# Later weight loads, and queries of the second batch loaded by token, in a one-core attention and MLP kernel

## The chip, the cores and the metric

The kernel runs on one core of one Trainium2 chip. The metric is the device time of one execution in microseconds (us). The core has five engines that run side by side, each in the order of its own program: TensorE (PE in the profile, its weight loads PEld), VectorE (DVE), ScalarE (ACT), GpSimd (POOL) and SyncE (SP). DMA transfers are issued from SyncE's and GpSimd's queues, and all of them run on the same 16 DMA engines.

## The reference

There are 4 batches of 8 heads, 768 tokens and 64 dimensions. The tokens are cut into 8 blocks of 96. A small matrix per head, made doubly stochastic by five Sinkhorn rounds, mixes the key and value blocks; each query block then attends to its mixed key block alone. The result, as 768 tokens of 512 channels, goes through a residual MLP: one matrix over tokens, one pair of matrices over channels.

```python
P = sort_net
for _ in range(5):
    P = P - np.max(P, axis=-1, keepdims=True)
    P = np.exp(P)
    P = P / (np.sum(P, axis=-1, keepdims=True) + 1e-09)
    P = P / (np.sum(P, axis=-2, keepdims=True) + 1e-09)
k_sorted = np.einsum('bhij,bhjcd->bhicd', P, k_b)      # v_sorted in the same way
scores = scale * np.matmul(q_b, k_sb.transpose(0, 1, 2, 4, 3))
attn = softmax(scores)                                 # per row, written out in the reference
x = np.matmul(attn, v_sb)                              # then heads side by side: (4, 768, 512)
a1 = alpha1 * x + beta1
u = x + lam * np.einsum('ts,bsd->btd', w_tok, a1)
a2 = alpha2 * u + beta2
out = u + lam * (np.maximum(a2 @ w_ch1, 0.0) @ w_ch2)
```

## The kernel before

**Order.** Every engine's instructions keep the order in which the program emits them (lines 55 to 77). Dependencies between engines, and the reuse of buffers, are guarded by semaphores that the framework sets. A tile is taken from a pool under a tag with a fixed number of copies; a new tile of a tag waits until the last reader of the tile whose place it takes is done, also when that reader stands later in the program than the new tile.

**Start-up (lines 96 to 319 and 900 to 989).** GpSimd issues the loads of batch 0: q in slabs (`load_slabs`, line 117: a partition holds 12 tokens of one head in one piece), v in halves of 64 partitions (`load_halves`, line 122), k in slabs, then the four loads of `w_tok` (lines 156 to 170). Meanwhile VectorE and ScalarE make the Sinkhorn matrix (lines 302 to 319); the table `beside` (line 293) lists what is emitted after each of the five rounds: `heads` (two small constant tables on ScalarE), the turning of q by TensorE (`q_first`), its copies out (`q_out`), and `slow`, a matmul on zeros that only keeps TensorE running. From line 900 the sorted v is laid out by copies (`v_sort`) on GpSimd and ScalarE and mixed, then k, then scores (`score`), weighted sums (`pv_first`), the permutation and transposition of `w_tok` (`permute`, `prep_wtok`), and the token matrix of batch 0 (`first_mm`, `first_turn`). `first_turn` needs `brow`, the product of beta and lam in one row (line 944), copied to three further partitions by SyncE.

**Batches.** A batch's MLP runs in two halves (`hf` 0 and 1) of 384 tokens. A half has 16 hidden units (`h_unit`, kind "h") and then product steps (`ch_unit` or `ch_pair`, kind "c"). The work of the next batch's attention is hung between them: `put(b, hf, kind, n, f)` emits `f` after hidden unit or product step `n` of half `hf` of batch `b`. The attention of batch 1 lies in batch 0: the mixing of v and k (`mix_v`, `mix_k`) at the end of the first half, scores and weighted sums (`pv`) between the hidden units of the second half, from (0, 1, "h", 0) on. The mixing of batch 2 lies in the product steps (0, 1, "c", 0) to (0, 1, "c", 7).

**Loads of the later batches.** `load_kv` (line 195) loads v, then k, in halves, into the tag `raw`, which has two copies. `load_q` (line 185) loads q into the tag `qn`, which has one: batch 1 in slabs (two DMAs), batches 2 and 3 by tokens (six DMAs; a partition is a token, in 64-element pieces per head). q of batch 1 is turned by TensorE in `q_turn_late` (line 538), 24 matmuls of 64 by 64 and two copies by VectorE for each of four groups of two heads, at product steps 4, 5, 7 and 8 of batch 0's first half; q of batches 2 and 3 is turned by transposing DMAs on SyncE (`q_cross`). `loads(2)` stands at (0, 0, "c", 11). It begins with a one-element copy on GpSimd from Vs (`gate`), which waits until the mixed v of batch 1 is back from its way through DRAM (`bounce_v` out, `back_v` in).

## Time and profile before

| | us |
|---|---|
| runs | 256.35, 256.37, 257.83 (median 256.37) |
| profiled execution | 256.33 |
| its span | 254.6 |
| DVE busy | 174.1 |
| ACT busy | 155.7 |
| POOL busy | 46.1 |
| q of batch 1, turned by TensorE: first to last group | 58.2 to 64.5 |
| `gate` of batch 2's loads | 69.2 |
| first mix of batch 2's v | 84.8 |

All the engine times are from one profiled execution and count from the start of its span. In the profile's lines, `out<-in` are the program's tile names without numbers, and all work has line 65, the helper that records every instruction, so lines are told apart by tile names: `raw` is a tile of v or k, `qn` and `q8b` of q, `wt` and `wp` of w_tok, `sc_ps` of scores, `x_ps` of weighted sums, `mix_ps` and `kmix_ps` of the mixing, `h_ps` of hidden units, `ch_ps` of products. A line of the timeline gives start, duration, engine, operation, tiles and shapes, the count, and in brackets the idle time before it with what ended it. A line of windows gives the stretch, its length, busy time and instructions of PE, PEld, DVE, ACT and POOL, the granted clock of TensorE, the DMA share and GB/s.

### The profile page before, as it was taken

To read this page: it belongs to the slowest core of one execution; us is meant where nothing else is said; L and a number is where in the kernel's file an instruction comes from. 1 tells how busy PE (TensorE), PEld (TensorE's weight loads), DVE (VectorE), ACT (ScalarE), POOL (GpSimd) and SP (SyncE) were. 2 spreads that over 40 slices of the span, in tenths; PEclk is the share of its full clock that TensorE was granted. 3 is DMA by queue.
4 is the path that set the end of the run, shared out by engine and by line. 5 is a ranking of instruction groups with operands and counts; after the bars stand their busy time and mean duration, and the time that the engine had idled before them with its cause. 6 is when DMAs were issued, how large, how long until landed. Compare 5 with 4: busy or idle time off the path is not lost.

```text
span 254.6 us, 6059 instructions
## 1 busy us (share of the span) xinstructions
PE 244.0 (96%) x2416; PEld 159.7 (63%) x2416; DVE 174.1 (68%) x461; ACT 155.7 (61%) x285; POOL 46.1 (18%) x70
## 2 busy tenths in 40 slices
PE   7897999999999999999999999999999999999994
PEld 2475765555465545556765797558756875686783
DVE  5884588667379868279896685398978862462773
ACT  4796675567788679786564696878364005837400
POOL 8699604000082010191000010000000000000000
PEclk9997999999999999999999999999999999999999
DMA  5999999998999997999961179710203132111023
GB/s 98 202 210 192 207 205 210 216 179 197 165 179 180 131 209 124 178 159 164 136 161 39 31 189 127 141 23 0 85 0 66 50 115 45 21 41 44 0 85 82
DMA packets 61936, 31.09 MB, mean 122 GB/s; under 512 B 50562, under 2 KB 57618, under 8 KB 61908
## 3 DMA queue, kind: packets, MB, share of 16 engines
q0 software_dynamic: 20976, 16.91, 45.7%
q1 hardware_dynamic: 40836, 13.76, 32.0%
q8 instruction: 19, 0.31, 0.5%
q14 instruction: 9, 0.07, 0.1%
q10 hardware_dynamic: 96, 0.03, 0.1%
HBM read 32.79 MB, written 8.65 MB: 163 GB/s over the span
## 4 chain that ended last, share of the span: by engine, by line
PE 77%; DVE 9%; ACT 6%; DMA 3%; issue 2%; POOL 1%; DVEq 0%; ACTq 0%; POOLq 0%
PE h_ps L65 28%; PE tok_ps L65 12%; PE px L65 8%; PE ch_ps L65 8%; PE pz L65 6%; PE py L65 5%; DMA v<-in_v_dram 3%; PE x_ps L65 3%; DVE x L65 3%; PE sc_ps L65 2%; DVE sums L65 2%; PE kmix_ps L65 2%; PE mix_ps L65 2%; ACT kT L65 1%; ACT vd L65 1%
## 5 line engine op out<-in xcount | busy, mean ns | idle before, releaser
L65 PE MATMUL h_ps<-a2T,W1p 128*128 128x384 bf16 x512 | 93.4, 326 | 0.3 <-DVE a2T L65 0.3
L65 PEld LDWEIGHTS <-W1p 128*128 128x128 bf16 x512 | 47.8, 98 | 30.7
L65 ACT ACTIVATE hTa<-h_ps 128x384 f16<-128x384 f32 x64 | 31.2, 490 | 30.6 <-PE h_ps L65 29.5
L65 ACT ACTIVATE hTb<-h_ps 128x384 f16<-128x384 f32 x64 | 31.3, 489 | 8.7 <-PE h_ps L65 8.7
L65 DVE SCALAR_TENSOR_TENSOR u<-tok_ps,x 128x512 f32<-128x512 f32 x21 | 14.5, 692 | 27.0 <-PE tok_ps L65 27.0
L65 PE MATMUL tok_ps<-a,w_tokT 128*128 128x512 f16 x126 | 30.3, 379 | 0.0
L65 ACT CAST kT<-kmix_ps 64x512 f16<-64x512 f32 x36 | 25.7, 713 | 7.0 <-PE kmix_ps L65 6.5
L65 ACT ACTIVATE et<-sc_ps 96x768 f16<-96x768 f32 (+2 forms) x36 | 24.6, 736 | 2.4 <-PE sc_ps L65 2.4
L65 ACT CAST u<-u 128x512 f16<-128x512 f32 x21 | 13.0, 618 | 20.4 <-DVE u L65 20.4
L65 PEld LDWEIGHTS <-sums 128*128 128x128 f16 x216 | 21.1, 98 | 3.8 <-issue 0.7
L65 PEld LDWEIGHTS <-hTa 128*128 128x128 f16 x192 | 18.2, 98 | 6.6
L65 PEld LDWEIGHTS <-hTb 128*128 128x128 f16 x200 | 18.5, 98 | 6.1
L65 PEld LDWEIGHTS <-w_tokT 128*128 128x128 f16 x126 | 12.3, 98 | 13.1 <-DVE a L65 0.3
L65 DVE TENSOR_TENSOR x<-x_ps,rcb 96x512 f16<-96x512 f32 x24 | 16.5, 687 | 0.8
L65 DVE TENSOR_TENSOR sums<-hTa,hTb 128x512 f16<-128x512 f16 (+2 forms) x27 | 8.9, 330 | 10.3 <-ACT hTb L65 10.0
L65 PEld LDWEIGHTS <-et 96*128 96x128 f16 (+4 forms) x288 | 12.6, 103 | 2.7
L65 DVE SCALAR_TENSOR_TENSOR ost<-px,u 128x256 f32<-128x256 f32 x27 | 11.3, 419 | 3.4 <-PE px L65 3.4
L65 PE MATMUL x_ps<-Vs,et 96*128 96x65 f16 (+4 forms) x288 | 13.5, 199 | 0.0
L65 PE MATMUL ch_ps<-W2p,hTa 128*128 128x512 f16 x48 | 11.9, 380 | 0.0
L65 PE MATMUL ch_ps<-W2p,hTb 128*128 128x512 f16 x48 | 11.7, 379 | 0.0
L65 POOL DMA_DIRECT2D qn<-in_q_dram x12 | 10.7, 915 | 5.2 <-DMA raw<-in_v_dram 4.8
L65 PE MATMUL sc_ps<-qT,kT 64*128 64x96 f16 (+1 forms) x256 | 10.0, 210 | 1.5 <-DVE x L65 0.7
(140 smaller groups left out, 351.2 us busy)
## 6 DMA issues: line engine op xcount, KB each, us to landing
out_dram<-ost SPq DMA_DIRECT2D x23, 192.0 KB, 2.4
raw<-in_v_dram POOLq DMA_DIRECT2D x6, 384.0 KB, 8.4
raw<-in_k_dram POOLq DMA_DIRECT2D x6, 384.0 KB, 10.8
Vs<-vscr SPq DMA_DIRECT2D x3, 768.0 KB, 7.9
W1p<-in_moe_w_ch_dram POOLq DMA_DIRECT2D x4, 512.0 KB, 11.6
W2p<-in_moe_w_ch_dram POOLq DMA_DIRECT2D x4, 512.0 KB, 15.6
qn<-in_q_dram POOLq DMA_DIRECT2D x12, 128.0 KB, 11.1
vscr<-mixed POOLq DMA_DIRECT2D x4, 384.0 KB, 5.0
```

Of the source, the lines that this page charges most:

```text
L65: ins = getattr(self.eng, name)(*args, **kwargs)
```

## The change

It has five parts. The loads of `w_tok` become a function that is called after GpSimd's value sorts. The table `beside` is reordered: `heads` one round later, one `slow` moved behind the mixing of keys. The product for `brow` and its copies move behind the loads of alpha, beta and lam, two W1 loads and the first permutation; `pv_first(1)` moves ahead of group 2's scores. v of batch 1 is loaded ahead of the last part of W2, and the scaling of that part moves from hidden unit 12 to 15. And q: batch 1's is loaded by tokens, as batches 2 and 3 are, and turned by six 128-column transposes and one copy per group, the first at product step 10, the others after hidden units 1, 3 and 5 of the second half; for batch 2, q is issued ahead of v and k.

```diff
--- before.py
+++ after.py
@@ -154,19 +154,19 @@
     load_halves(v8, v[0])
     load_slabs(k8, k[0])
     wt16 = []
-    for half in range(2):
-        t_ = att.tile([128, 3, S], F16, name="wt16", tag=("sums", "qn")[half], bufs=(2, 1)[half])
-        for lo, n in ((0, 96), (TAIL, 32)):
-            pool.dma_start(
-                t_[lo // 6:lo // 6 + n],
-                moe_w_tok[lo + 3 * half * n:lo + 3 * (half + 1) * n, :].rearrange("(tt p) s -> p tt s", p=n),
-            )
-        wt16.append(t_)
-        if half == 0:
-            pool.memset(VD[:, :, HB:64], 0.0)
-            pool.memset(
-                KT0[:].rearrange("p g i (th t) -> p (g i th) t", th=2)[:, :, HB:64].bitcast(FT), 0.0
-            )
+
+    def load_wt():
+        for half in range(2):
+            t_ = att.tile([128, 3, S], F16, name="wt16", tag=("sums", "qn")[half], bufs=(2, 1)[half])
+            for lo, n in ((0, 96), (TAIL, 32)):
+                pool.dma_start(
+                    t_[lo // 6:lo // 6 + n],
+                    moe_w_tok[lo + 3 * half * n:lo + 3 * (half + 1) * n, :].rearrange("(tt p) s -> p tt s", p=n),
+                )
+            wt16.append(t_)
+
+    pool.memset(VD[:, :, HB:64], 0.0)
+    pool.memset(KT0[:].rearrange("p g i (th t) -> p (g i th) t", th=2)[:, :, HB:64].bitcast(FT), 0.0)
 
     def v_sort(lo, hi, eng):
         eng(VD[:, lo:hi, 0:HB], v8[:, :, lo:hi].rearrange("p t d -> p d t"))
@@ -183,17 +183,15 @@
     qn_of = {}
 
     def load_q(b):
-        if b == 1:
-            qn_of[b] = att.tile([128, H4, 12 * D], F16, name="q8b", tag="qn", bufs=1)
-            return load_slabs(qn_of[b], q[b])
         qn_of[b] = att.tile([128, NT, H, D], F16, name="qn", tag="qn", bufs=1)
         for kt in range(NT):
             pool.dma_start(
                 qn_of[b][:, kt, :, :], q[b, :, kt * 128:(kt + 1) * 128, :].rearrange("h p d -> p h d"),
             )
 
-    def load_kv(b):
-        for kv, src in ((1, v), (0, k)):
+    def load_kv(b, *kvs):
+        for kv in kvs or (1, 0):
+            src = (k, v)[kv]
             raw = att.tile([128, HB, D], F16, name="raw", tag="raw", bufs=2)
             load_halves(raw, src[b])
             raw_of[(b, kv)] = raw
@@ -254,7 +252,7 @@
     def q_turn(b, g, ps):
         if g == 0:
             qT_of[b] = att.tile([128, H4, S], F16, name="qT", tag="qT", bufs=1)
-        return turn_slab(qn_of[1] if b else q8, lambda r, g: ident16[r, r], g, "q_ps", ps)
+        return turn_slab(q8, lambda r, g: ident16[r, r], g, "q_ps", ps)
 
     def q_copy(b, g, ps, half, eng):
         eng(
@@ -291,11 +289,11 @@
             q_copy(0, g, qps[g], half, act.copy)
 
     beside = {
-        0: [heads, lambda: q_first(0), lambda: q_first(1)],
-        1: [lambda: slow(1), lambda: q_first(2)],
-        2: [lambda: q_out(0), lambda: slow(1)],
-        3: [lambda: q_out(1), lambda: q_out(2, 0), lambda: q_first(3), lambda: slow(1)],
-        4: [lambda: q_out(2, 1), lambda: q_out(3), lambda: prep_ab2(psb), lambda: gaps()],
+        0: [lambda: q_first(0), lambda: q_first(1)],
+        1: [heads, lambda: slow(1), lambda: q_first(2)],
+        2: [lambda: q_out(0), lambda: q_first(3)],
+        3: [lambda: q_out(1), lambda: slow(1)],
+        4: [lambda: q_out(2), lambda: q_out(3), lambda: prep_ab2(psb), lambda: gaps()],
     }
     slow(2)
     warm(1)
@@ -536,16 +534,25 @@
         )
 
     def q_turn_late(g):
-        ps = q_turn(1, g, psb)
-        q_copy(1, g, ps, 0, dve.tensor_copy)
-        q_copy(1, g, ps, 1, dve.tensor_copy)
+        if g == 0:
+            qT_of[1] = att.tile([128, H4, S], F16, name="qT", tag="qT", bufs=1)
+        ps = psb([128, S], F16, "qt_ps")
+        for kt in range(NT):
+            pe.transpose(
+                ps[:, kt * 128:(kt + 1) * 128],
+                qn_of[1][:, kt, 2 * g:2 * g + 2, :].rearrange("p a d -> p (a d)"), ident16[:],
+            )
+        dve.tensor_copy(qT_of[1][:, g, :], ps[:])
 
     gate = const([1, 1], F16, "gate")
 
     def loads(b):
         pool.tensor_copy(gate[:], Vs[0:1, 0, 0:1])
+        if b == 2:
+            load_q(b)
         load_kv(b)
-        load_q(b)
+        if b > 2:
+            load_q(b)
 
     mixed = {}
 
@@ -900,9 +907,11 @@
     mix_values(0, psb)
     warm(1)
     mix_keys(0, psb)
+    slow(1)
     v_sort(48, 64, pool.tensor_copy)
     v_sort(40, 48, pool.tensor_copy)
     v_sort(32, 40, pool.tensor_copy)
+    load_wt()
     for n in range(4):
         v_sort(8 * n, 8 * n + 8, act.copy)
 
@@ -941,19 +950,21 @@
     score(0, 1, 0, psb, 1)
     score(0, 1, 1, psb)
     prep_scales()
-    pool.tensor_tensor(brow[0:1, :], bet1[:], lam1[:], ALU.mult)
-    for j in range(1, 4):
-        sp.dma_start(brow[32 * j:32 * j + 1, :], brow[0:1, :])
     pool.dma_start(alphaB[:], moe_alpha1.partition_broadcast(128))
     pool.dma_start(betaB[:], moe_beta1.partition_broadcast(128))
     pool.dma_start(lamB[:], moe_lam.partition_broadcast(128))
     for g in range(2):
         pool.dma_start(W1p[:, :, g * 512:(g + 1) * 512], w1v[:, :, g * 512:(g + 1) * 512])
     permute(0, pool.tensor_copy, 0, 6)
+    pool.tensor_tensor(brow[0:1, :], bet1[:], lam1[:], ALU.mult)
+    for j in range(1, 4):
+        sp.dma_start(brow[32 * j:32 * j + 1, :], brow[0:1, :])
     for g in range(2, 4):
         pool.dma_start(W1p[:, :, g * 512:(g + 1) * 512], w1v[:, :, g * 512:(g + 1) * 512])
     permute(1, pool.tensor_copy, 0, 6)
     for g in range(4):
+        if g == 3:
+            load_kv(1, 1)
         pool.dma_start(W2p[:, g * 4:(g + 1) * 4, :], w2v[:, g * 4:(g + 1) * 4, :])
     moe_start(0)
     a1_of[0] = moep.tile([128, 8, C], F16, name="a1", tag="a1", bufs=1)
@@ -963,9 +974,9 @@
     for g, kp in ((2, kp2), (3, kp3)):
         k_copy(0, g, kp, 0, copy)
         k_copy(0, g, kp, 1, act.copy)
+    pv_first(1)
     score(0, 2, 0, psa)
     score(0, 2, 1, psb)
-    pv_first(1)
     score(0, 3, 0, psb)
     score(0, 3, 1, psa)
     for ks in range(4):
@@ -984,7 +995,7 @@
     first_turn(2, psa)
     scale_affine(betaB)
 
-    load_kv(1)
+    load_kv(1, 0)
     load_q(1)
     pool.memset(Vs[0:BLK, :, D:GRP], 1.0)
 
@@ -1020,7 +1031,7 @@
             put(0, 0, "h", 15, lambda: bounce_v(1))
             put(0, 0, "c", 2, lambda: back_v(1))
             for g in range(H4):
-                put(0, 0, "c", (4, 5, 7, 8)[g], lambda g=g: q_turn_late(g))
+                put(0, min(g, 1), *(("c", 10), ("h", 1), ("h", 3), ("h", 5))[g], lambda g=g: q_turn_late(g))
             put(0, 0, "c", 11, lambda: loads(2))
             seq = [("s", 0), ("s", 1), ("s", 2), ("p", 0), ("s", 3), ("p", 1), ("p", 2), ("s", 4), ("p", 3), ("s", 5),
                    ("p", 4), ("s", 6), ("p", 5), ("s", 7), ("p", 6), ("p", 7)]
@@ -1058,7 +1069,7 @@
         put(b, 0, "h", 4, lambda b=b: moe_cross(b, 1))
         put(b, 0, "c", 2, lambda b=b: moe_affine(b, 1))
 
-    for g, m in enumerate((10, 11, 12, 12)):
+    for g, m in enumerate((10, 11, 12, 15)):
         put(0, 0, "h", m, lambda g=g: scale_weights(g))
     for n, at_ in enumerate(((0, 1, "c", 4),) * 3 + ((0, 1, "c", 5),) * 3 + ((0, 1, "c", 6),) * 2):
         put(*at_, lambda n=n: block_weights(n))
```

## The prediction

> **What bounds the kernel now.** I read the page first, then windows over the stages the change touches, then the timelines of GpSimd, SyncE and TensorE there. Two lines of the page, busy time and granted clock:
>
> ```profile
> PE 244.0 (96%) x2416; PEld 159.7 (63%) x2416; DVE 174.1 (68%) x461; ACT 155.7 (61%) x285; POOL 46.1 (18%) x70
> ...
> PEclk9997999999999999999999999999999999999999
> ```
>
> TensorE is busy for 244.0 of 254.6 us and works in program order. From about 22 us on, whatever it waits for lengthens the run, and what other engines save does not shorten it. The one dent is in the first 27 us; the windows there (engine busy time, then granted clock, DMA share, GB/s):
>
> ```profile
> 19.80:21.20 1.40, 0.00 (x0) 0.00 (x0) 1.02 (x2) 0.50 (x2) 1.40 (x2) 1.00 1.21 200
> ...
> 23.00:26.30 3.30, 3.30 (x55) 2.89 (x51) 1.50 (x4) 2.60 (x6) 3.30 (x4) 0.51 1.18 223
> ```
>
> TensorE stood still for 1.4 us, and soon afterwards ran 3.3 us at a granted clock of 0.51. In the stretch 19.3 to 22.6, one such length before, it was busy 0.44 + 0 + 0.94 + 0.07 = 1.45 of 3.3 us (44%). In 9 to 13 us it was busy about 80% and stayed at 1.00.
>
> The batch-2 loads, on GpSimd's queue:
>
> ```profile
> 69.19 0.18 POOL L65 COPY gate<-Vs 1x1 f16<-1x1 f16 x1 [25.74 <-DMA Vs<-vscr]
> ...
> 69.80 1.08 POOL L65 DMA_DIRECT2D raw<-in_v_dram  x2 [0.43 <-issue]
> 70.86 1.06 POOL L65 DMA_DIRECT2D raw<-in_k_dram  x2
> 71.87 3.61 POOL L65 DMA_DIRECT2D qn<-in_q_dram  x4
> 76.48 0.88 POOL L65 DMA_DIRECT2D qn<-in_q_dram  x1 [0.99 <-DMA raw<-in_v_dram]
> 78.85 0.87 POOL L65 DMA_DIRECT2D qn<-in_q_dram  x1 [1.49 <-DMA raw<-in_v_dram]
> ```
>
> The gate opens when batch 1's values are back in Vs; then v, k and q go out in that order. Their users on TensorE, from its timeline:
>
> ```profile
> 73.42 0.82 PE L65 MATMUL h_ps<-a2T,W1p 128*128 128x384 bf16 x4
> ...
> 84.78 0.59 PE L65 MATMUL mix_ps<-raw,bigM 128*128 128x512 f16 x2
> ...
> 87.80 0.61 PE L65 MATMUL kmix_ps<-bigP,raw 128*128 128x128 f16 x8
> ```
>
> The mix of v at 84.78 comes 14.4 us after the second v load was issued (70.34), the mix of k at 87.80. This cover is what the change spends. The last view is the stage before it, where q of batch 1 is turned today:
>
> ```profile
> 58.23 0.57 PE L65 MATMUL q_ps<-ident,q8b 64*64 64x64 f16 x24
> ...
> 68.88 0.34 PE L65 MATMUL sc_ps<-qT,kT 64*128 64x96 f16 x7 [0.43 <-ACT kT L65]
> ```
>
> **Start-up.** The four w_tok loads (0.56 to 0.69 us of issue each, 2.5 in sum) move behind GpSimd's three value sorts, which end at 15.1. GpSimd idled 2.2 us before those sorts, so the issue was free and now is not: the alpha, beta and lam rows and W1 go out about 2.5 us later. The transfers themselves are in one line: q landed at 6.0 and 8.0, v at 10.0 and 11.9, k at 14.8 and 16.6, w_tok at 19 to 22. So v, which starts the critical sorts at 12.0, was not held by w_tok behind it: 0 gained (bounds 0 and the 2.2 us that GpSimd waited for v; I take 0, as v's landing follows q's at q's pace). A load issued at 15.1 moves its first bytes about 2 us later (q: issued 1.27, traffic from 3), so the DMA engines stay idle for about 0.5 us after k and every later load shifts by that. First w_tok lands near 20; the permutation starts at 20.9 instead of 19.9 and ends at 23.1, while its transposes run at 25.4: hidden by 2.3 us. If that cover went, each us late would cost a us. The brow product (1.26 us) moves behind that permutation, to 24.4; its three copies need 1.9 us to issue and 4.9 to land, so the last lands near 30.5, against its first use at 30.24: +0.3, bounds 0 and 1.5 (copies each a full 4.9 after a late product).
>
> The heads leave the Sinkhorn chain (its Exp waited for them from 4.12 to 4.69), but v at 11.9 still ends last: 0. One 1.1-us filler matmul is moved behind the mixing of keys, where TensorE waits for sorted v until 12.98: 0 (bounds 0 and 0.6). The weighted sum of group 1 goes ahead of group 2's scores and fills the 0.4-us wait before 22.54: -0.4. Start-up: **-0.1**.
>
> **Loads of batch 1.** v goes ahead of the last W2 part, which lands some 4 us later, near 50.5; its scaling starts at 53.8 today and its first matmul at about 56: hidden. q by tokens moves in 64-element pieces. The q loads of batch 2 show their pace: 155 GB/s in 80 to 86 us, against 207 around 35 us. For 0.79 MB this is 5.1 instead of 3.8 us, so q lands near 59 instead of 57.3. Its first transpose comes at about 64: hidden by 5 us. GpSimd issues six loads of 0.91 instead of two of 0.74 us, with nothing urgent behind them. The bounce of batch 1's v (SyncE, 55.05) and its way back (61.22, 7.9 us to landing) share the engines with q and may land 0 to 2 us after 69.1; the weighted sum that needs it comes at about 70.9: 0, bounds 0 and 1.
>
> **Turning q.** A group's 24 matmuls pushed the next product from 58.14 to 58.73, 0.59 us. Six transposes: three of w_tok's push the next matmul by 0.16 us (36.80 to 36.96), so 0.33 for six; with weight loads of 0.098 us fully exposed, 0.59. I take 0.4. Four groups leave the first product stage before its last mix of k: 4 x 0.59 = 2.36. ScalarE's key copies are freed as early (third set at 63.6, second set done at 63.4), so kT is complete at 66.5 instead of 68.8 and scores start 2.36 earlier. Three groups return in the next stage: 3 x 0.4 = 1.2. VectorE trades eight copies of 0.548 us, idle time there, for four of about 0.55 (w_tok's 384 columns took 0.29 to 0.36); three fall into 70 to 80 us, where it is busy 8.39 of 10 us, and 1.65 us of work fits 1.61 of room: +0.2, bounds 0 and 1. Sum: -2.36 + 1.2 + 0.2 = **-1.0**. TensorE would reach the mix of v at 83.8.
>
> **q ahead of v and k in batch 2.** This adds a wait. The buffer of q has one copy, and its last reader is now batch 1's fourth turn, after the sixth hidden unit: 73.42 + 0.65 - 2.36 + 0.8 + 0.4 + 0.2 = 73.1 us. GpSimd stands at the first q load until then, and queued behind it are five q loads, then v, then k. Six issues take 5.4 us; the second v load goes out 6.0 us after 73.1 instead of at 70.34: 8.8 us later. TensorE has 83.8 - 73.1 = 10.7 us. Landing of v from issue: 5.1 us (shortest raw load) to 8.4 (median), so 11.1 to 14.4 us after 73.1: a stall of 0.4 to 3.7. By the whole transfer: v, k and q took from 69.8 until the traffic fell at 86,
>
> ```profile
> 85.00:86.00 1.00, 1.00 (x6) 0.49 (x5) 0.97 (x3) 0.59 (x1) 0.00 (x0) 1.00 3.39 144
> 86.00:87.00 1.00, 1.00 (x7) 0.45 (x5) 0.95 (x3) 0.72 (x2) 0.00 (x0) 1.00 0.36 23
> ```
>
> 16.2 us. Begun at 73.1 it ends at 89.3, now with k, needed at 86.8: a stall of 2.5. The two ways give 2.5 to 3.7; I take **3.0**, bounds 0.4 and 5 (a gate 1 us later as well). SyncE's transposes of q no longer wait for q, but batch 2's scores only begin at 102.8, so that gains nothing.
>
> **Sum.** -0.1 - 1.0 + 3.0 = +1.9 us on the profiled run's 256.33 (span 254.6 and 1.7 around it; the median shown is 256.37): **258.2 us**, if the stall leaves the clock alone.
>
> **Rivals.**
> B, half clock after the stall: a 3.0-us standstill in a 3.3-us stretch leaves TensorE busy for as little as 10%, or some 55% in each of two stretches if it straddles them; 44% was followed by 3.3 us at 0.51 above, 80% was not. TensorE is fully loaded in 87 to 91 us, so such a stretch costs 3.3 x 0.49 = 1.6 us: 259.8, slower. It decides once the stall takes over half of a stretch. [...]
>
> C, the early half-clock stretch vanishes: with the filled gap TensorE is busy about 1.9 of 3.3 us (57%) before 22.6, between the 44% and the 80%. Gain 1.6: 256.6.
>
> D, v and k land in time (5.1 us from issue, k close behind): 255.2. For it: loads of one queue landed strictly in turn at start-up. Against: the second v load took 8.4 us even when nothing of its queue but v was ahead.
>
> E, the later w_tok does not clear the way but starves the start: if the DMA engines idle until 18 to 19 us and brow lands late, start-up costs 2 to 2.5 us more: 260.5.
>
> **Chances.** A (forecast) 0.38, B 0.22, C 0.14, D 0.13, E 0.08, C and D together (253.6) 0.05. A's own range, from its bounds, is 256 to 260. The range reaches from the lower part of D to the upper part of E; C with D, the ends of D and E, and B with a longer stall are left out, about 2 in 10: **254.5 to 260.8**. About 1% (2.6 us) is what a measurement of this kernel can tell from no change. Faster by more, below 253.8: C with D and the low edge of D, 0.07. Slower, above 258.9: B, E and the upper quarter of A, 0.39. Within: 0.54.
>
> **What would show it.** In the changed profile: GpSimd's gate near 69 and its first batch-2 q load not before 73; second v load near 79; TensorE idle 2 to 4 us at the first mix of v or k of batch 2, released by a load; a slice below 9 in the clock row near 88 us for B, none near 24 us for C; scores of batch 1 near 66.5; brow's copies near 24.5 and the first turn within 0.5 us of 30.2. I am wrong if that idle time is under 1 us, or if the first hidden unit, at 33.0 today, moves by over 1 us.

## The result, and the profile after

The changed kernel takes **264.98 us** (median of 6 runs, 263.59 to 265.82) against 256.48 us (median of 6 runs, 256.28 to 257.83) for the kernel before: a ratio of 1.031, 95% interval 1.028 to 1.034. That is 8.5 us slower. The prediction was 258.2 us, with 260.8 as its upper end: too fast by 6.8 us, and outside the range. The profiled execution took 264.54 us, with a span of 262.8 us.

On the page, the busy times and the clock row answer to the two lines shown of before:

```profile
PE 245.6 (93%) x2344; PEld 160.0 (61%) x2344; DVE 173.2 (66%) x457; ACT 155.9 (59%) x285; POOL 50.2 (19%) x74
...
PEclk9999859999999979999999999999999999999999
```

TensorE has 1.6 us more of busy time in a span that is 8.2 us longer, so most of the loss is standing still and the rest slower work, and the clock row has two dents, near 34 us and near 95 us. Before had one, near 24 us, which the changed kernel has not; about what such a dent costs (1.68 us behind the mix of v, below) is gained in the first row of the table below. The times at which TensorE reaches the same work in the two profiled executions split the 8.2 us. "First turn" is the matmul that reads `brow`; "arrival" is the time at which TensorE would have started without the wait.

| stretch of TensorE | before | after | difference |
|---|---|---|---|
| start of the span to the arrival at the first turn | 30.24 | 28.75 | -1.49 |
| wait for `brow` | 0 | 3.47 | +3.47 |
| first turn to first hidden unit | 2.75 | 5.05 | +2.30 |
| first hidden unit to first product | 20.39 | 20.42 | +0.03 |
| first product to the arrival at the mix of batch 2's v | 31.40 | 30.56 | -0.84 |
| wait for that v | 0 | 3.44 | +3.44 |
| mix of v to the next token matmul | 4.33 | 6.01 | +1.68 |
| from there to the end of the span | 165.49 | 165.10 | -0.39 |
| sum | 254.6 | 262.8 | +8.2 |

There are two waits of about 3.5 us, and behind each a stretch of half clock. The first, in TensorE's timelines of the kernel before and then of the changed kernel (start, duration, engine, operation, tiles, shapes, count, and in brackets the idle time with its releaser):

```profile
30.24 0.33 PE L65 MATMUL turn_ps<-rrow,brow 128*128 128x384 f16 x1
...
32.99 0.49 PE L65 MATMUL h_ps<-a2T,W1p 128*128 128x384 bf16 x2
```

```profile
28.42 0.33 PE L65 MATMUL turn_ps<-ident,x 128*128 128x128 f16 x3
32.22 0.48 PE L65 MATMUL turn_ps<-rrow,brow 128*128 128x384 f16 x1 [3.47 <-DMA brow<-brow]
...
37.27 1.14 PE L65 MATMUL h_ps<-a2T,W1p 128*128 128x384 bf16 x3
```

The first turn starts at 32.22 and not at 30.24, after 3.47 us of waiting for the copies of `brow`, and the first hidden unit is at 37.27 instead of 32.99. Windows of the changed kernel there and at the second wait (stretch, length, busy time and instructions of PE, PEld, DVE, ACT and POOL, granted clock, DMA share, GB/s):

```profile
30.00:31.00 1.00, 0.00 (x0) 0.00 (x0) 0.00 (x0) 0.00 (x0) 1.00 (x3) 1.00 1.32 205
31.00:32.00 1.00, 0.00 (x0) 0.00 (x0) 0.00 (x0) 0.00 (x0) 0.98 (x2) 0.71 1.24 201
...
37.00:38.00 1.00, 1.00 (x6) 0.49 (x4) 0.00 (x0) 0.94 (x2) 0.00 (x0) 0.50 1.24 207
38.00:39.00 1.00, 1.00 (x9) 0.64 (x8) 0.79 (x2) 0.40 (x2) 0.00 (x0) 0.87 1.24 206
...
90.00:91.00 1.00, 0.00 (x0) 0.00 (x0) 0.96 (x4) 0.00 (x0) 0.00 (x0) 1.00 1.01 193
...
94.00:95.00 1.00, 1.00 (x4) 0.39 (x3) 0.00 (x0) 0.82 (x1) 0.00 (x0) 0.50 1.10 161
```

At 30 to 32 us TensorE does nothing; the clock falls before it starts again and is back at 38.3 (0.87 in the last of these windows), some 6.8 us after it fell, 6.0 of them behind the start of the first turn. At 89 to 91 us it again does nothing, and from 93 to 96 us it runs at 0.50 again. GpSimd's timelines, of before and then of the changed kernel, have the cause of the first wait and the order of loads behind the second, and SyncE's has the copies:

```profile
15.09 1.26 POOL L65 TENSOR_TENSOR brow<-bet,lam 1x512 f16<-1x512 f32 x1
...
19.91 2.24 POOL L65 COPY wp<-wt 128x1728 f16<-128x1728 f16 x2
```

```profile
15.10 2.46 POOL L65 DMA_DIRECT2D wt<-in_moe_w_tok_dram  x4
...
20.82 0.75 POOL L65 DMA_DIRECT2D W1p<-in_moe_w_ch_dram  x1 [0.83 <-DMA wt<-in_moe_w_tok_dram]
21.56 2.24 POOL L65 COPY wp<-wt 128x1728 f16<-128x1728 f16 x2
23.75 1.26 POOL L65 TENSOR_TENSOR brow<-bet,lam 1x512 f16<-1x512 f32 x1
...
74.50 0.18 POOL L65 COPY gate<-Vs 1x1 f16<-1x1 f16 x1 [20.56 <-DVE repv_ps L65]
78.01 1.75 POOL L65 DMA_DIRECT2D qn<-in_q_dram  x2 [3.33 <-PE x_ps L65]
79.95 3.50 POOL L65 DMA_DIRECT2D qn<-in_q_dram  x4 [0.18 <-issue]
83.41 1.12 POOL L65 DMA_DIRECT2D raw<-in_v_dram  x2
```

```profile
25.04 2.11 SPq L65 DMA_DIRECT2D brow<-brow  x3
```

The w_tok loads occupy GpSimd for 2.46 us from 15.10, and a W1 load then waits 0.83 us until one of them has landed, so the permutation starts at 21.56 instead of 19.91. The `brow` product, behind it now, ends at 25.0; SyncE issues three copies until 27.15. The profile gives a landing for the first two only, 6.5 and 6.0 us after their issue (before: 5.0 and 4.8); the third, issued at 26.52, had landed when the first turn started at 32.22, so 5.7 us later at the most. Further down, the gate opens at 74.50, the first q load of batch 2 waits another 3.33 us, and v goes out at 83.41 where it went at 69.80. What that q load waits for is the last reader of q's buffer: the fourth turn of batch 1 ends at 77.71, 0.30 us before the load starts, and the same 0.30 us lie between the two with q's part alone and with `brow` or w_tok early. The profile names `x_ps`, a weighted sum that ran just behind that turn.

The second wait, from TensorE's and VectorE's timelines of the changed kernel:

```profile
87.38 1.03 PE L65 MATMUL ch_ps<-W2p,hTa 128*128 128x512 f16 x4
91.69 0.59 PE L65 MATMUL mix_ps<-raw,bigM 128*128 128x512 f16 x2 [3.28 <-DVE a L65]
```

```profile
91.13 0.56 DVE L65 TENSOR_TENSOR a<-x,alphaB 128x768 f16<-128x768 f16 x1
```

Four product matmuls take 0.87 us before the mix when nothing waits, so it would have come at 88.25; it came at 91.69. The profile names VectorE as its releaser, since that scaling of `a` ends at 91.69. This is a coincidence, as a kernel below shows (the change with v and k of batch 2 loaded first): in its timelines of TensorE and VectorE the mix of v starts 2.9 us before that same scaling.

```profile
87.51 0.59 PE L65 MATMUL mix_ps<-raw,bigM 128*128 128x512 f16 x2
```

```profile
90.44 0.56 DVE L65 TENSOR_TENSOR a<-x,alphaB 128x768 f16<-128x768 f16 x1
```

The second half of v was issued at 83.9 and landed 7.6 us later, at about 91.5: that is the releaser. With `brow` early the same wait, 3.43 us until 91.75, is put down to the load of v.

### The profile page after: what moved, and what is told of

The parts are those of the page before. It is cut to its first block, busy times and chain, and to the rows that moved or that the text cites. A ratio compares the mean times of both kernels' runs of the same rounds, so it can differ in the third digit from the quotient of the medians.

```text
span 262.8 us, 5916 instructions
## 1 busy us (share of the span) xinstructions
PE 245.6 (93%) x2344; PEld 160.0 (61%) x2344; DVE 173.2 (66%) x457; ACT 155.9 (59%) x285; POOL 50.2 (19%) x74
## 4 chain that ended last, share of the span: by engine, by line
PE 74%; DVE 10%; DMA 7%; POOL 3%; ACT 2%; issue 2%; SPq 1%; DVEq 0%; POOLq 0%
PE h_ps L65 27%; PE tok_ps L65 11%; PE px L65 8%; PE ch_ps L65 7%; PE pz L65 6%; PE py L65 5%; DVE x L65 4%; DMA v<-in_v_dram 3%; DMA wt<-in_moe_w_tok_dram 2%; DMA brow<-brow 2%; PE x_ps L65 2%; PE mix_ps L65 2%; PE sc_ps L65 2%; PE kmix_ps L65 2%; DVE a L65 1%
## 5 line engine op out<-in xcount | busy, mean ns | idle before, releaser
L65 POOL DMA_DIRECT2D qn<-in_q_dram x18 | 15.9, 906 | 6.7 <-PE x_ps L65 3.3
L65 ACT CAST mixed<-mix_ps 128x1024 f16<-128x1024 f32 x9 | 9.2, 1017 | 8.7 <-PE mix_ps L65 8.7
L65 PE MATMUL ch_ps<-W2p,hTb 128*128 128x512 f16 x48 | 12.7, 400 | 0.0
```

The costliest lines, as they stand in the source:

```text
L65: ins = getattr(self.eng, name)(*args, **kwargs)
```

## The experiments

All ratios are to the kernel before, run on the same chip beside the kernel; absolute times of different groups are not compared. The kernels compute everything that the changed kernel computes. "Start part" means all of the change but q's part. The diffs are shortened: `...` stands for lines left out, and some statements of several lines stand on one.

### brow early

The change with the product for `brow` and its copies back where they were:

```diff
     prep_scales()
+    pool.tensor_tensor(brow[0:1, :], bet1[:], lam1[:], ALU.mult)
+    for j in range(1, 4): sp.dma_start(brow[32 * j:32 * j + 1, :], brow[0:1, :])
     pool.dma_start(alphaB[:], moe_alpha1.partition_broadcast(128))
...
     permute(0, pool.tensor_copy, 0, 6)
-    pool.tensor_tensor(brow[0:1, :], bet1[:], lam1[:], ALU.mult)
-    for j in range(1, 4): sp.dma_start(brow[32 * j:32 * j + 1, :], brow[0:1, :])
```

> The changed kernel with the brow product and its three copies put back ahead of the alpha, beta and lam loads; all else as changed (w_tok late). Theory A (the late brow row stops TensorE for 3.5 us in front of the first turn, and the half clock that follows costs about 2.3 more): 5.8 us less than the changed kernel's 265.0, so 259.2 (258 to 260.5), and the first hidden unit near 31.5 to 32 instead of 37.3. Rival (the later w_tok and the hole in the DMA traffic at 15 to 18 us delay the start in any case): less than 2 us is gained, 263 or more.

Measured: 264.38 us, ratio 1.025 (1.018 to 1.032). The start behaves as it should if `brow` is the cause; the time, expected 5.8 us lower, hardly moves. TensorE's timeline of this kernel:

```profile
28.89 0.33 PE L65 MATMUL turn_ps<-rrow,brow 128*128 128x384 f16 x1
...
31.64 0.49 PE L65 MATMUL h_ps<-a2T,W1p 128*128 128x384 bf16 x2
...
65.85 0.23 PE L65 MATMUL qt_ps<-ident,qn 128*128 128x128 f16 x1 [0.89 <-DMA qn<-in_q_dram]
...
67.53 0.29 PE L65 MATMUL qt_ps<-ident,qn 128*128 128x128 f16 x1 [0.85 <-DMA qn<-in_q_dram]
67.62 1.91 PE L65 MATMUL ch_ps<-W2p,hTb 128*128 128x512 f16 x4
...
70.72 0.34 PE L65 MATMUL sc_ps<-qT,kT 64*128 64x96 f16 x8
```

There is no wait at the first turn (28.89), and the first hidden unit comes at 31.64, 5.6 us earlier than in the changed kernel. By the first score of batch 1, at 70.72, all of it is gone (changed kernel: 70.47). TensorE waits 0.93 us for v and 0.48 us for k of batch 1, then three times for q of batch 1 (0.89, 0.37, 0.85), and after that it runs at 0.50: four product matmuls at 67.62 take 1.91 instead of 1.03 us. The last q load goes out at 53.82, since GpSimd first waits 2.18 us for a W2 part to land, and it lands 13.7 us later, at 67.5. So the late start had hidden a second lateness, that of batch 1's loads.

### v and k first

The change with `load_kv(b)` ahead of `load_q(b)` again in `loads`:

```diff
-        if b == 2:
-            load_q(b)
         load_kv(b)
-        if b > 2:
-            load_q(b)
+        load_q(b)
```

> The changed kernel with batch 2's loads in the old order, v and k ahead of q; all else as changed. Theory A (v queued behind q, which waits for the last turn of batch 1's q, stops TensorE for 3.45 us at batch 2's first mix of v, and the half clock after it costs 1.7): 5.1 us less, 259.9 (259 to 261). Rival (VectorE, which works without a pause from 78 to 92 us and whose last scaling ends exactly when the mix starts, is what the mix waits for, by its accumulator banks): the wait stays, 263.5 or more.

Measured: 260.41 us, ratio 1.012 (1.007 to 1.016). The wait at the mix of v is gone (87.51, no idle time), no half clock follows, and the next token matmul comes at 91.84 instead of 97.70. The start is as late as in the changed kernel (first hidden unit 36.78, after 3.78 us of waiting for `brow`). Against the change itself, 1.9 of the 3.1 per cent are gone, about the 5.1 us expected. Behind the mixing a smaller wait appears, 1.28 us for `a2T` at 104.97.

### Both

The last two edits together, on the change:

```diff
+    pool.tensor_tensor(brow[0:1, :], bet1[:], lam1[:], ALU.mult)
...
     pool.dma_start(alphaB[:], moe_alpha1.partition_broadcast(128))
...
         load_kv(b)
+        load_q(b)
```

> Both edits together: brow early, and v and k ahead of q. Theory A, by the sum: 265.0 - 5.8 - 5.1 = 254.1 (252.5 to 255.5), which is below the kernel before (256.4), because the turned q in its new place gains about 1 us and the early half-clock stretch at 23 to 26 us stays away (1.5). Rival (the two costs hide one another, or the early half-clock stretch comes back): 255.5 to 258.

Measured: 261.47 us, ratio 1.015 (1.010 to 1.019): no better than the second alone, and 1.0 per cent better than the first alone. The first turn (31.40) and the mix of v (86.34) are without a wait. The 254.1 us expected, and even the rival's 255.5 to 258, were too fast. What is left, against before, is a first hidden unit that comes 1.16 us later (34.15), two waits for q of batch 1 (0.49 and 0.72 us), and a wait until 104.75, 2.23 us for `a2T`, the input of batch 1's second half of hidden units, with half clock behind it from 106.3 to 109.7.

### The same waits with TensorE kept running

The change with three filler matmuls on zeros ahead of the first turn, and three ahead of the mix of v:

```diff
+    slow(3)
     first_turn(0, psb)
...
+                if b == 2 and n == 0:
+                    put(p - 1, 1, "c", 0, lambda: slow(3))
```

> The changed kernel with three matmuls on zeros (about 1.1 us each) put into each of the two waits, ahead of the first turn and ahead of batch 2's first mix of v. The waits stay as long; TensorE only does not stand still in them. Theory A (after a wait of over 3 us TensorE runs at half clock for one 3.4-us stretch, and this costs 2.3 and 1.7 us): the clock stays at 1.00 behind both, about 261.0 (260 to 262). Rival (the half clock costs little, since data is late there anyway): 264 to 266.

Measured: 262.58 us, ratio 1.021 (1.015 to 1.026), and the granted clock is 1.00 over the whole span. TensorE's timeline at the first wait:

```profile
29.23 2.74 PE L65 MATMUL warm_ps<-wz 128*128 128x512 f32 x6
...
33.46 0.32 PE L65 MATMUL turn_ps<-rrow,brow 128*128 128x384 f16 x1 [1.33 <-DMA brow<-brow]
...
36.20 0.49 PE L65 MATMUL h_ps<-a2T,W1p 128*128 128x384 bf16 x2
```

The fillers turn 3.47 us of idle time into 1.33; the first turn is no earlier (33.46), but from there to the first hidden unit it takes 2.74 us instead of 5.05. So 2.3 us of the changed kernel's start are half clock and nothing else. At the mix the clock matters less: the three mixes of v are over earlier, but then k makes TensorE wait until 95.91 (0.69 us), and the next token matmul comes at 97.22 instead of 97.70. Both half clocks together are worth about 1 per cent (1.031 against 1.021, intervals apart), less than the 4.0 us expected.

### The two parts apart

First the kernel before with q's part alone: loads by token, the turns and their places, q first for batch 2.

```diff
-        if b == 1: return load_slabs(qn_of[b], q[b])
...
+        ps = psb([128, S], F16, "qt_ps")
+        for kt in range(NT): pe.transpose(...)
+        dve.tensor_copy(qT_of[1][:, g, :], ps[:])
...
+        if b == 2: load_q(b)
         load_kv(b)
...
-    put(0, 0, "c", (4, 5, 7, 8)[g], lambda g=g: q_turn_late(g))
+    put(0, min(g, 1), *(("c", 10), ("h", 1), ("h", 3), ("h", 5))[g], lambda g=g: q_turn_late(g))
```

> The kernel before with the q part of the change alone: q of batch 1 by tokens, turned by 128-column transposes in the new places, and q ahead of v and k in batch 2. Start-up, w_tok and the order of batch 1's loads stay. Theory B (three separate limits; batch 1's q by tokens lands only at about 64 to 66 us, and the changed kernel hid that behind its late start): waits of 0 to 3 us at the first turn, the stall of 3 to 3.5 us and the half clock (1.7) at batch 2's first mix of v, and 1 us gained by the new places: 5 to 7 us slower than before. Rival (the q part is good by itself and is spoiled only by the late start): within 2 us of before.

Measured: 260.99 us, ratio 1.013 (1.008 to 1.018). GpSimd's and TensorE's timelines:

```profile
71.12 0.18 POOL L65 COPY gate<-Vs 1x1 f16<-1x1 f16 x1 [20.12 <-DVE bigP L65]
73.87 1.76 POOL L65 DMA_DIRECT2D qn<-in_q_dram  x2 [2.57 <-PE x_ps L65]
...
79.27 1.11 POOL L65 DMA_DIRECT2D raw<-in_v_dram  x2
```

```profile
88.34 0.59 PE L65 MATMUL mix_ps<-raw,bigM 128*128 128x512 f16 x2 [4.07 <-DMA raw<-in_v_dram]
```

The start is that of before (first hidden unit 33.06), and q of batch 1 comes in time, without a wait. The first score of batch 1 comes at 66.23, 2.0 us before that of before. Then the first q load of batch 2 is issued at 73.87, v at 79.27, and TensorE stands for 4.07 us at the mix of v, with half clock behind it (0.50 from 89.50 to 92.91). The time is 3 to 4 us longer than before's, between the 5 to 7 expected and the rival's 2.

Then the change with q's part undone, that is, the start part alone (the diff above, turned round, on the changed kernel):

> The changed kernel with the q part undone: the start-up of the change (w_tok late, brow late, heads and filler moved, weighted sum of group 1 ahead) and v of batch 1 ahead of the last W2 part, with q in slabs, turned in the old places, v and k first. Theory B: the start loses 4.3 us at the first product, as in the changed kernel, and all of it stays: about 4.3 us slower than before (3 to 5.5). Rival (what the start loses was idle time for later loads anyway): under 2 us slower.

Measured: 260.11 us, ratio 1.011 (1.006 to 1.015). The first hidden unit comes at 36.65. In its profiled execution the standstill is not at the first turn but before it: 1.85 us ahead of a weighted sum, for which the profile names no releaser, then half clock to 34 us; the first turn, at 33.65, found `brow` ready. The two copies with a recorded landing took 5.5 us; at that pace the last, issued at 26.9, landed at 32.4 (an estimate). So `brow` is about as late here as in the change, but something else held TensorE longer in this execution. The part costs about 2.8 us, a little under the 3 to 5.5 expected. The two parts' intervals add to 1.4 to 3.3 per cent; the whole change has 2.8 to 3.4.

### q first alone, and the weighted sum alone

The kernel before with only the order of batch 2's loads changed:

```diff
+        if b == 2: load_q(b)
         load_kv(b)
-        load_q(b)
+        if b > 2: load_q(b)
```

> The kernel before with one edit: in batch 2, q is issued ahead of v and k. Its buffer is free early there, since batch 1's q is turned before 65 us. Theory B (the stall comes from the pair: q in front, and q's buffer held until the sixth hidden unit): the second v load goes out near 76 us, lands near 84, and the mix at 84.8 waits under 1 us: within 1 us of before. Rival (q in front of v and k costs a stall by itself, as six issues of 0.9 us and 5 us of transfer stand in front): 2 us or more slower, with a wait at the first mix of v.

Measured: 256.83 us, ratio 0.999 (0.996 to 1.002). The q loads go out at 71.81, 0.37 us behind the gate, v at 77.05, and the mixes wait 0.95 us for v and 0.71 us for k. In that execution (258.13 us) the next token matmul comes 1.84 us later than before; in the median nothing is to be seen. Here, where q's buffer was free, q first cost nothing that the median shows.

The kernel before with only `pv_first(1)` ahead of group 2's scores:

```diff
+    pv_first(1)
     score(0, 2, 0, psa)
     score(0, 2, 1, psb)
-    pv_first(1)
```

> The kernel before with one edit: the weighted sum of group 1 ahead of group 2's scores. If this is what removed the half-clock stretch at 23 to 26 us in the changed kernel: 1 to 2 us faster than before, first turn near 28.8 instead of 30.2. Rival (the stretch depends on where its window falls, or on the order of the Sinkhorn stage): within 0.5 us of before, and the stretch still there in the profile.

Measured: 256.80 us, ratio 0.998 (0.995 to 1.001). In its profiled execution there is no early half clock, but there is none either in that of the kernel just above, which leaves the start alone. The early dent comes and goes between executions.

### w_tok early

The change with the four w_tok loads back in their old place, `brow` still behind the permutation:

```diff
-    def load_wt():
-        for half in range(2):
+    for half in range(2):
...
     v_sort(32, 40, pool.tensor_copy)
-    load_wt()
```

> The changed kernel with the four w_tok loads alone put back to their old place; brow stays behind the first permutation. Theory C (the 2.5 us of issue that w_tok's loads put in front of the permutation, and the 2-us hole in the DMA traffic, are what makes brow late): permutation near 19, brow's product near 21.5, its copies landed by 29, the wait at the first turn under 1 us instead of 3.5; the first hidden unit near 32. But, as with brow early, batch 1's loads may then be what is late: 259 to 262. Rival (the place of brow behind the permutation is enough, w_tok does not matter): the wait stays at 3 us or more, 264 to 266.

Measured: 261.51 us, ratio 1.016 (1.010 to 1.023). GpSimd's and TensorE's timelines:

```profile
20.41 2.24 POOL L65 COPY wp<-wt 128x1728 f16<-128x1728 f16 x2
22.61 1.27 POOL L65 TENSOR_TENSOR brow<-bet,lam 1x512 f16<-1x512 f32 x1
```

```profile
30.64 0.33 PE L65 MATMUL turn_ps<-rrow,brow 128*128 128x384 f16 x1
...
33.38 0.49 PE L65 MATMUL h_ps<-a2T,W1p 128*128 128x384 bf16 x2
```

The permutation starts at 20.41 and the product ends at 23.9, 1.1 us earlier than in the changed kernel. The two copies with a recorded landing took 5.5 and 5.2 us; if the last, issued at 25.3, took 5.2 too, it landed at 30.5 instead of 32.2. The first turn does not wait, but TensorE also comes to it later than in the changed kernel, at 30.64 instead of 28.75, since it waited 1.55 us at 20.8 for ScalarE. With the changed kernel's arrival, 1.7 to 1.8 us of wait would be left, about half. So, by this estimate, w_tok's place accounts for 1.7 us of the copies' lateness, `brow`'s own place for the rest. The wait for v of batch 2 stays (3.93 us), and the time is close to that of q's part alone (1.016 and 1.013, intervals overlapping).

### All three put right

The change with w_tok early, `brow` early, and v and k first (the diffs of "Both" and "w_tok early" together):

> The changed kernel with three things undone: w_tok early, brow early, v and k ahead of q in batch 2. What is left of it is q by tokens and turned late, the weighted sum of group 1 ahead, v of batch 1 ahead of the last W2 part. Theory C: all three large waits are gone; what remains is a wait of 1 to 2 us at batch 1's second hidden stage (near 103 us), since q of batch 2 lands late and SyncE's transposes of u stand behind those of q, against 1 to 2 us gained: 256 to 258, about the kernel before. Rival (q by tokens lands too late for its first turn once the start is not late): a wait of 2 us or more near 64 us and 259 or more.

Measured: 257.46 us, ratio 1.003 (1.000 to 1.005). Against "Both", which differs in w_tok's place alone, this is 1.2 per cent: w_tok's 2.5 us cost about 3 us even when `brow` is early. The first hidden unit is in the same place in both (34.07 and 34.15). The difference is in the loads behind w_tok: GpSimd's last q load of batch 1 goes out at 50.84 instead of 53.91 and q no longer makes TensorE wait, and the wait at batch 1's second half of hidden units shrinks from 2.23 to 0.65 us, with no half clock behind it. Windows from 14 to 50 us, of "Both" and then of this kernel:

```profile
14.00:50.00 36.00, 32.11 (x536) 21.38 (x529) 24.63 (x52) 24.05 (x50) 22.41 (x30) 1.00 1.12 189
```

```profile
14.00:50.00 36.00, 32.80 (x535) 22.47 (x529) 24.26 (x52) 24.12 (x50) 20.77 (x27) 0.95 1.19 207
```

With w_tok late, the DMA engines move 189 instead of 207 GB/s in these 36 us, 0.65 MB less, which at 207 GB/s are 3.1 us of transfers: the loads behind come about that much later. The changed kernel moves 190 GB/s there, before 207.

### The turns earlier

The kernel before with q's part, with the four turns at product steps 10 and 11 and hidden units 0 and 1, instead of 10 and hidden units 1, 3 and 5, which frees q's buffer earlier; with q first:

```diff
-   put(0, min(g, 1), *(("c", 10), ("h", 1), ("h", 3), ("h", 5))[g], lambda g=g: q_turn_late(g))
+   put(0, g // 2, *(("c", 10), ("c", 11), ("h", 0), ("h", 1))[g], lambda g=g: q_turn_late(g))
```

> The q part of the change on the start-up of before, with q ahead of v and k in batch 2, as in the run of the q part alone (3.7 us slower than before, a stall of 4.1 us), but turned at product steps 10 and 11 and after hidden units 0 and 1. Only the place of the buffer's last reader differs. Theory C (the reader holds GpSimd's queue): first q load of batch 2 right after the gate (70 to 71 us) instead of at 73.9, the wait at the first mix of v 1 to 2 us instead of 4.1, no half clock behind it, 257 to 258.5. Rival (six small q loads in front of v are the cost, whatever the buffer): wait of 3 us or more, 260 or more.

Measured: 258.81 us, ratio 1.007 (1.003 to 1.010). GpSimd's and TensorE's timelines:

```profile
71.53 1.75 POOL L65 DMA_DIRECT2D qn<-in_q_dram  x2 [0.59 <-PE x_ps L65]
...
76.94 1.09 POOL L65 DMA_DIRECT2D raw<-in_v_dram  x2
```

```profile
85.68 0.59 PE L65 MATMUL mix_ps<-raw,bigM 128*128 128x512 f16 x2 [1.98 <-DMA raw<-in_v_dram]
```

The first q load goes out at 71.53 instead of 73.87, v 2.3 us earlier, and the wait falls from 4.07 to 1.98 us, with 0.67 more for k. So a buffer that is free earlier takes away about half of the second loss, and the six issues ahead of v, with a wait of 1.98 us left, are about the other half. The time, expected at 257 to 258.5, is just above it.

The same with v and k first, by the edit of "v and k first":

> The kernel before with q of batch 1 by tokens and turned by 128-column transposes, but at product steps 10 and 11 and after hidden units 0 and 1, so that its buffer is free near 68 us, before the gate opens; v and k ahead of q in batch 2; start-up as before. Theory C: nothing waits for the buffer, the 2 us gained in the product stage stay in part: 255 to 256.3 where before is 256.4, 1 to 0.2 us faster. Rival (the turns crowd VectorE in front of the first weighted sums, or q lands too late): 257 or more.

Measured: 257.38 us, ratio 1.003 (1.000 to 1.006). The mix of v comes at 83.63 without a wait, 1.15 us earlier than before, though the first hidden unit was 0.45 us later: the new turning gains 1.6 us here. It is not in the time, which was expected at 255 to 256.3, because of SyncE and TensorE later:

```profile
83.97 11.05 SPq L65 DMA_TRANSPOSE qT<-qn  x6
...
96.20 3.81 SPq L65 DMA_TRANSPOSE uT<-u  x3
```

```profile
101.69 1.19 PE L65 MATMUL h_ps<-a2T,W1p 128*128 128x384 bf16 x4 [1.88 <-DVE a2T L65]
```

q of batch 2 is transposed by SyncE in 11.05 us (before: 8.30, from 82.97); the transposes of `u`, which stand behind it on the same queue, start at 96.20 instead of 94.46, and TensorE waits 1.88 us for `a2T`, which is made from them. In the four kernels with this wait (this one, "v and k first", "Both", "All three put right") the next hidden unit starts 5.5 us after the transposes of `u` start, whether that is at 96.20 or at 99.49; where there is no wait it starts over 6.2 us after them (before: 6.34). That the late transposes of `u` cause the wait is read from this and from the queue's order, and was not tried by itself. No kernel here is measurably faster than the kernel before.

## Why the prediction was wrong

**The brow term failed; with the half clock behind it, it carries about half of the loss.** The prediction gave +0.3 us, bounds 0 and 1.5, to `brow` behind the permutation. It measured 3.47 us of wait. Its parts: the permutation, forecast at 20.9, started at 21.56, because a W1 load on the same queue first waited 0.83 us for w_tok; the product then ended at 25.0 instead of 24.4; the copies took longer, 6.5 and 6.0 us for the two on record instead of 4.9, so that the last landed near 32.2 and not 30.5; and TensorE came to the first turn at 28.75 and not at 30.24. Together 0.3 + 1.7 + 1.5 = 3.5 us; the forecast landing, 0.3 us behind the use, left no room for any of it. Why the copies were slower is open: the traffic was 201 to 240 GB/s at 26 to 32 us, and before, with copies of 4.8 to 5.0 us, it was 200 to 221 at 16 to 21 us. The upper bound let the product be late and the copies slow, but not the load between, nor an earlier arrival of TensorE. That arrival differs between executions: the first transpose of w_tok starts between 23.9 and 26.4 in the profiles here, in no order that the edits explain, and at 25.4 in that of before. ("brow early" and "Both" have the same program up to the loads of batch 2, and 24.3 and 25.3.) A landing that is late sets the time of the first turn wherever TensorE arrives. About half of the loss is what the split of one profile shows; mending this term alone gave back little (1.025 instead of 1.031), since the loads of batch 1 were then late.

**The half clock was weighed at one wait and left out at the other.** Rival B had the right mechanism and the right size: 3.4 us of standstill, then 3.4 us at 0.50, +1.68 us where 1.6 was forecast. The prediction considered it at the mix of v alone, because only there did it expect a stall; at the start it cost another 2.30 us. Its condition, a standstill over half of a 3.3-us stretch, was the author's estimate between the 44% and the 80% of the kernel before; it roughly holds in the runs. The stretches of 3.41 us that end where the clock falls, in the changed kernel (the first and the fourth line; the second and third are the two that follow the first):

```profile
28.02:31.43 3.41, 0.73 (x7) 0.36 (x5) 0.52 (x1) 0.58 (x2) 3.41 (x7) 1.00 1.28 207
31.43:34.84 3.41, 2.62 (x30) 2.13 (x31) 1.23 (x3) 0.67 (x1) 1.33 (x3) 0.50 1.24 206
34.84:38.26 3.42, 3.42 (x15) 1.73 (x14) 1.84 (x4) 1.92 (x3) 0.00 (x0) 0.50 1.24 206
...
89.46:92.87 3.41, 1.19 (x6) 0.61 (x7) 2.68 (x7) 0.56 (x1) 0.00 (x0) 1.00 1.00 189
```

TensorE was busy for 21% and 35% of them. In the stretch that ended at such a fall it was busy for 46% in before, 47 and 19% with `brow` early, 10% with v and k first, 45% with both, 34% and 20% with q's part and with w_tok early (at the mix of v), 46% with the start part alone, 50% with all three put right, 38 and 50% with the turns early; one fall, at 14.4 us with q's part alone, came after 66% and fits no such bound. A stretch that took in most of a wait, but was busy for 51% (the 1.98 us of the turns early with q first), 55% (the 1.88 us with v and k first) or 66% (with the fillers, counted from that kernel's own fall behind its last work), was followed by none. The first of these:

```profile
84.00:87.41 3.41, 1.73 (x9) 0.82 (x10) 3.27 (x8) 1.01 (x1) 0.00 (x0) 1.00 0.97 186
```

The bound is not sharp. The clock of the changed kernel came back at 38.26 and fell at 92.87, and these 54.61 us are 16 times 3.413. Counted in steps of 3.413 us from its own kernel's fall at 22.49, the stretch shown is at 83.93 to 87.34 and 49% busy; with q's part alone the 47% of 82.67 to 86.08, which takes in the first 1.8 us of the wait for v, were followed by no fall, only the 34% behind them. And with q first alone TensorE was busy for 44% of 19.39 to 22.80 and the clock stayed at 1.00. So the runs have falls behind stretches that were busy for 10 to 50% (once 66%), and none behind others at 44 to 66%; what decides where the two overlap they do not show. The half clock lasted 3.41 us in all cases but one: that of the changed kernel's first wait was still there after a stretch at 77% and gone after the next, at 100%, 6.83 us in all.

**The stall at the mix of v was right.** The first q load of batch 2 was put at 73.1 us; with the old start it went out at 73.87. The second v load was to leave 6.0 us after it and left 5.9 us after it. The stall was 3.44 us in the change and 4.07 with q's part alone, for a forecast of 3.0 with bounds 0.4 and 5. Rival D is refuted: the second half of v landed 7.6 us after its issue in the change and 8.4 us with q's part alone.

**Turning q was right.** First scores 2.36 us earlier were forecast, 2.0 were seen with q's part alone. A net 1.0 was forecast at the mix of v; from the first hidden unit to there TensorE needed 0.8 us less in the change (its wait taken out) and 0.6 with q's part alone, and 1.6 less with the turns early and v first.

**v ahead of the last W2 part was hidden,** as forecast: the stretch from the first hidden unit to the first product is the same (20.42 and 20.39). The heads' and the filler's places were not tried by themselves.

**Loads of batch 1 "hidden by 5 us" was wrong, at no cost in the change.** q lands at 67.5 us with `brow` early, not at 59: GpSimd spreads the six issues over 12 us (41.70 to 53.82) because it waits between them for earlier loads to land, where before it issued k's two and q's two in one go from 40.76 to 43.2, and the transfers then took 13.7 to 18.9 us. In the change itself the late start covered this. The prediction checked each part against the old schedule, so it could not see that one lateness hides another; for the same reason the gain from mending one of them was given back.

**C and E.** The early dent was absent in the changed kernel, as C says, but it is absent as well from the profiles of kernels that leave that place alone, and the weighted sum ahead makes no difference: C's mechanism is not shown. E's starved start was half right: the DMA engines fell to 37, 59 and 103 GB/s at 15 to 18 us (before: 212, 209 and 208), and again to 146 and 68 at 23 to 25 us (before: 243 and 211), while GpSimd was busy with the permutation and the product. The prediction put the hole at about 0.5 us for every later load; by the bytes moved it is about 3 us, and w_tok's place costs about 3 us through the loads behind it, more than E's 2 to 2.5. In sum, up to the next token matmul: forecast -0.1 - 1.0 + 3.0 = +1.9; measured +4.3 (start) - 0.8 + 3.4 + 1.7 (second half clock) = +8.6.

## What to carry over

Where several parts of a change delay the same consumer, add their delays on the queue that carries them before pricing any of them, and put the sum against a cover that is measured from the consumer's earliest arrival, not its old one: w_tok's delay alone cost the first turn nothing (`brow` early) and `brow`'s own move alone nothing or up to 1.8 us, by when TensorE arrived; together they cost 3.5 us and a half clock. Count also the bytes that the DMA engines do not move while nothing is issued: between "Both" and "All three put right" it was 0.65 MB, 3.1 us at 207 GB/s, and the last q load of batch 1 went out 3.07 us later. A standstill of 1.85 us (the start part alone) had half clock behind it, one of 1.98 us (the turns early, q first) had none: price one of that length or more at its length and up to 1.7 to 2.3 us on top, what the half clock cost behind the two waits here, if TensorE is the bound after it. And before a load is moved ahead of others, ask who still reads its buffer: q first cost 1.7 to 2.7 us of waiting for v and k with a buffer that was free early, and 3.4 to 4.1 us for v with one held by a late reader, with half clock behind it.

## What was not expected of the hardware

- The half clock behind the first wait lasted two stretches of 3.41 us, with TensorE busy for 77% of the first and 100% of the second; with `brow` early, behind the wait for v, it lasted one stretch, with 81% busy.
- Six loads of 128 KB in 64-element pieces took 13.7 to 18.9 us from issue to landing beside other traffic (q of batch 1 with `brow` early), where loads of the same kind issued first in batch 2, at 78 to 83 us of the changed kernel, took 3.3 to 4.3 us.
- By the profile's releasers, GpSimd stopped between loads until an earlier load had landed: 0.83 us ahead of W1 for w_tok, 0.88 and 1.27 us ahead of q for v and W2 in the changed kernel, 9 us in sum ahead of q with `brow` early. Whether the framework or the chip asks for it, the runs do not tell.
- Copies of one row of 512 elements (two of the three have a landing on record) landed 4.8 and 5.0 us after issue before, 6.0 and 6.5 us after it in the changed kernel, and 6.1 and 8.0 us with `brow` early.
